# A convolution and expert kernel on one core: scatters, first step and small operations placed otherwise

## The chip, the core and the metric

One core of a Trainium2 chip runs the whole kernel. A core has five engines, each with an instruction list of its own that it takes in order: TensorE (PE: matmuls, and PEld: the loads of their weights), VectorE (DVE), ScalarE (ACT), GpSimd (POOL) and SyncE (SP), which here issues loads and stores. [...] The metric is the time of the kernel in device microseconds (us), as the median of several executions.

## The reference

The input `x` (8 × 3584 × 192) is weighted over the last seven rows, with softmax weights for each of eight groups of 24 columns. Each of the 28672 rows of the result goes through the one of eight experts that has the largest gate product.

```python
def _attn_ref(x, weight_gen) -> np.ndarray:
    w = weight_gen - np.max(weight_gen, axis=-1, keepdims=True)
    w = np.exp(w)
    w = w / (np.sum(w, axis=-1, keepdims=True) + 1e-09)
    ...
    out = np.einsum('bshk,bskhg->bshg', w, x_unf)

def _moe_ref(x, w_gate, w1, w2) -> np.ndarray:
    logits = x @ w_gate
    expert_idx = np.argmax(logits, axis=1)
    ...
    for e in range(E):
        mask = expert_idx == e
        xe = x[mask]
        h = np.maximum(xe @ w1[e], 0.0)
        ye = h @ w2[e]
        out[mask] = gate_w[mask, None] * ye
```

## The kernel before

The kernel has two halves that run side by side. The **producing half** takes the rows in 16 chunks of 14 rows per partition (1792 rows). For each chunk VectorE makes the softmax weights (`soft_a`: maximum and difference, L324 and L326; ScalarE's exponential, L328; `soft_b`: sums, reciprocal and product, L361 to L370) and the convolution (13 pairs of halves, L387 and L392). The rows are then written as a high and a low part: ScalarE the high (`tops`, L401), VectorE the low (`halves`, L414). TensorE transposes them (`turn`, L428, 42 transposes; ScalarE copies them to `xt`, L429) and multiplies them by the gate (`products`, L437, 42 small matmuls). VectorE finds the expert of each row (`route1`, L451 to L464) and the number of rows for each expert of each partition, `cnt`; TensorE adds these up (`counts`, L479 and L480, with ScalarE's exponential of the gate values, `lg`, L478), and VectorE makes the position of each row in the experts' lists (`route2`, L503 to L519; `ge` is the sum of the exponentials and becomes the gate factor) and the tables of blocks (L542 and on). POOL then scatters the 14 rows of each partition to those positions in the memory `scr` (L491).

The **consuming half** takes blocks of 256 or 128 rows of one expert out of `scr`. SP loads the expert's weights `wa` (L622, L623) and `wb` (L654), the block's rows transposed, `xb` (L631), and their numbers, `mt` (L639). A block has four or two **steps**: TensorE makes 10 matmuls of the first product (L675 to L679), ScalarE `hh` from it (relu, L682), and the rest `hl` is made by VectorE (L692) or by TensorE and ScalarE (L689, L690). The second product (L709) follows some steps later, then ScalarE's `y` (L717) and POOL's scatter to the output (L718).

Ahead of both lies the preparation of the weights (to about 125 us): `gram` and `scales` find a scale for each expert, `high`, `split` and `low_sum` write the weights in two parts, and SP stores them to `wsa` and `wsb` (L288, L292, L296), from where the blocks load them. `first_rows` issues `xb` and `mt` of the very first block, `first_weights` its `wa`.

A planner that is written out by hand sets the order of the instructions: `produce` walks through slots `o` of each chunk `c` and adds the time `t` of VectorE's work; `consume` adds a step whenever its own time is due. `state["pe"]` is the time that the producing half takes on TensorE, which pushes the next step back. Tables such as `EARLY` and `THIRD` say in which slot each part comes. While the slots of chunk `c` run, the routing of chunk `c` − 1 is done; chunk numbers in this text count from 0. `PACED` is the first chunk whose scatters are tied to the steps: each such scatter waits for the `hh` of one step.

Of the kernel before, what the change touches and what calls it, by code (L numbers as in the profile page):

```python
# [19 lines left out]
E, F = 8, 1024  # L20
# [14 lines left out]
OPS = 2 * K - 1  # L35
WW = 7 * F + 2
WA, WB2 = 4160, 3136
PACED = 14
ZERO = dict(tops=0, halves=2, turn=3, per=1, products=8, route1=10, counts=12, route2=13, soft_a=11, soft_b=7, size=10)
FIRST = dict(tops=-1, halves=-1, turn=-1, per=6, products=-1, route1=2, counts=2, route2=3, soft_a=6, soft_b=10, size=8)  # L40
EARLY = dict(tops=-1, halves=1, turn=2, per=2, products=4, route1=6, counts=8, route2=9, soft_a=7, soft_b=10, size=11)
THIRD = dict(tops=-1, halves=0, turn=0, per=3, products=2, route1=3, counts=4, route2=5, soft_a=8, soft_b=10, size=11)
SECOND = dict(tops=-1, halves=-1, turn=-1, per=6, products=-1, route1=-1, counts=-1, route2=0, soft_a=6, soft_b=10, size=8)
END = 2.1
LONE = {1: 6, 2: 2}
WB = 4
SB = 5
# [33 lines left out]
def conv_moe_kernel(ctx: ExitStack, tc: tile.TileContext, x, wgen, wg_in, w1, w2, out):  # L81
# [151 lines left out]
    def prep_units():  # L233

        sqs = {}

        def gram(e):
            po = ps2.tile([P, 512], F32, name="po")
            for k in range(2):
                hi = ptiles[e][:, k, :].bitcast(BF16).rearrange("p (f z) -> p f z", z=2)[:, :, 1]  # L240
                for q in range(NW // P):
                    m = hi[:, q * P:q * P + P]
                    PE.matmul(po[:, k * P:k * P + P], lhsT=m, rhs=m, start=k == 0 and q == 0, stop=k == 1 and q == NW // P - 1)
            sqs[e] = po

        def norms(e):
            sq = small.tile([P, 2], F32, name="wsq", bufs=3)
            for k in range(2):
                gj = small.tile([P, P], F16, name="gj")
                A.activation(out=gj, in_=sqs[e][:, k * P:k * P + P], func=AF.Relu, scale=2.0 ** (-2 * (LW1, LW2)[k]), accum_out=sq[:, k:k + 1])  # L250
            PE.matmul(sqs[e][:, 256:258], lhsT=onef, rhs=sq, start=True, stop=True)

        def scales(e):
            with tc.high_priority(offset=PRIO3):
                scale_of(sqs.pop(e)[:, 256:258], ws[:, 2 * e:2 * e + 2], wi[:, 2 * e:2 * e + 2], V, WTOP)

        wts, stored = {}, {}

        def high(e, k):
            t = ptiles[e]  # L260
            sc = ws[:, 2 * e + k:2 * e + k + 1]
            si = small.tile([P, P], F32, name="si", bufs=3)
            A.activation(out=si, in_=idf, func=AF.Copy, scale=sc)
            wt = stg[0].tile([P, 2 * NW + 2], F16, name="wt", bufs=SB)
            A.activation(out=wt[:, 0:NW], in_=t[:, k, :], func=AF.Copy, scale=sc)
            if k:
                A.activation(out=wt.bitcast(F32)[:, NW:NW + 1], in_=wi[:, 2 * e:2 * e + 1], func=AF.Copy, scale=wi[:, 2 * e + 1:2 * e + 2])
            wts[e, k] = wt, si

        def low(e, k):  # L270
            t = ptiles[e]
            wt, si = wts.pop((e, k))
            for q in range(3):
                p1 = ps1.tile([P, 512], F32, name="p1")
                PE.matmul(p1, lhsT=si, rhs=t[:, k, q * 512:q * 512 + 512], start=True, stop=False)  # L275
                PE.matmul(p1, lhsT=negi, rhs=wt[:, q * 512:q * 512 + 512], start=False, stop=True)
                A.activation(out=wt[:, NW + q * 512:NW + q * 512 + 512], in_=p1, func=AF.Copy)
            stored[e, k] = wt

        def low_sum(e, k):  # L280
            wt, _ = wts.pop((e, k))
            V.scalar_tensor_tensor(out=wt[:, NW:2 * NW], in0=ptiles[e][:, k, :], scalar=ws[:, 2 * e + k:2 * e + k + 1], in1=wt[:, 0:NW], op0=ALU.mult, op1=ALU.subtract)
            stored[e, k] = wt

        def store(e, k, l):
            wt = stored.pop((e, k)) if l else wts[e, k][0]
            if k:
                SP.dma_start(out=wsb[e, :, l * NW:(NW, 2 * NW + 2)[l]], in_=wt[:, l * NW:2 * NW + 2 if l else NW])  # L288
                if l and e + WB < E:
                    prep_load(e + WB)  # L290
                return
            SP.dma_start(out=wsa[e, :, (1, 3)[l] * F:(2, 4)[l] * F], in_=wt[:, l * NW:l * NW + F])  # L292
            for y in range(2 - l):
                for z in range(2):
                    o = (2, 0)[l] * F + 512 * z
                    SP.dma_start(out=wsa[e, 64 * y:64 * y + 64, o:o + 512], in_=wt[64 * z:64 * z + 64, l * NW + F:(l + 1) * NW])  # L296

        units, last = [(TW0, 0, gram, 0), (0, 1.1, norms, 0), (0, 0.0, scales, 0), (0, 1.9, high, 0, 0), (0, 0, store, 0, 0, 0), (TW0 + TWE, 0, gram, 1)], None
        for e in range(E):
            if e:  # L300
                units += [(0, 1.9, high, e, 0), (0, 0, store, e, 0, 0)]
            if last:
                units += [(0, 2.0, low, *last), (0, 0, store, *last, 1)]
            if e + 1 < E:
                units.append((0, 1.1, norms, e + 1))
            units += [(0, 2.1, high, e, 1), (0, 0, store, e, 1, 0), (0, 2.0, low, e, 0), (0, 0, store, e, 0, 1)]
            if e + 2 < E:
                units.append((TW0 + (e + 2) * TWE, 0, gram, e + 2))
            if e + 1 < E:
                units.append((0, 0.0, scales, e + 1))  # L310
            last = (e, 1)
        units[-1:-1] = [(0, 0, first_rows)]
        units += [(0, 0.0, low_sum, *last), (0, 0, store, *last, 1), (0, 0, first_weights)]
        for t, cost, f, *args in units:
            yield t, cost, f.__name__
            f(*args)
            if f is norms or f is scales:
                state["norm"] = f is norms


    def soft_a(c):
        wgt, n = tin[c]["wgt"], WID[c] * H
        mx = small.tile([P, T * H], F32, name="mx")[:, 0:n]
        V.tensor_reduce(out=mx, in_=wgt, axis=AX.X, op=ALU.max)  # L324
        yield 1.0
        V.tensor_tensor(out=wgt, in0=wgt, in1=mx.unsqueeze(2).to_broadcast([P, n, K]), op=ALU.subtract)  # L326
        with tc.high_priority(offset=PRIO2):
            A.activation(out=wgt, in_=wgt, func=AF.Exp)  # L328
        yield 1.0

    def size_a(c):
        xin = tin[c]["xin"]
# [110 lines left out]
    def route1(s):  # L443
# [14 lines left out]
        with tc.high_priority(offset=PRIO2):  # L458
# [5 lines left out]
            V.tensor_tensor_scan(out=inc.rearrange("p e t -> p (e t)"), data0=scm[n].rearrange("p e t -> p (e t)"),  # L464
                                 data1=oh.rearrange("p e t -> p (e t)"), initial=0.0, op0=ALU.mult, op1=ALU.add)
            cnt = small.tile([P, E], F16, name="cnt")
            if s < 2:
                V.tensor_copy(out=cnt, in_=inc[:, :, n - 1])
            else:
                A.activation(out=cnt, in_=inc[:, :, n - 1], func=AF.Copy)  # L470
# [26 lines left out]
    def route2(s):  # L497
# [3 lines left out]
        with tc.high_priority(offset=PRIO2):  # L501
            ge = small.tile([P, n], F32, name="ge")
            V.tensor_reduce(out=ge, in_=lg, axis=AX.X, op=ALU.add)  # L503
            if s < 2:
                V.tensor_scalar(out=ge, in0=ge, scalar1=1e-9, scalar2=d["sx"][:, 1:2], op0=ALU.add, op1=ALU.mult)
            else:
                A.activation(out=ge, in_=ge, func=AF.Copy, bias=1e-9)
                A.activation(out=ge, in_=ge, func=AF.Copy, scale=d["sx"][:, 1:2])
# [258 lines left out]
    def produce():  # L767
# [19 lines left out]

        for _ in soft_a(0):
            pass
        for e in range(WB):  # L790
            prep_load(e)
        load_chunk(1)
# [4 lines left out]
        for c in range(nchunk + 1):  # L797
# [4 lines left out]
            for o in range(-1, OPS + 1 + LONE.get(c, 0) // 2):  # L802
# [15 lines left out]
                if c == 2 and o == -1:  # L818
                    ta = prepare(1e9, ta)
                    state["begin"] = t + TLOAD  # L820
                    for d in soft_a(c):
                        t += d
                    ta += 0.9
                if c == 1 and o == -1:
                    for d in soft_b(c):
# [9 lines left out]
                    turn_ = turn(c - 1)  # L835
                for _ in range(at_o["per"]):
                    if turn_ and next(turn_, 0):
                        state["pe"] += 0.9
                        ta += 1.1
                if o == at_o["products"] and c:  # L840
                    products_ = products(c - 1)
                for _ in range(1 if at_o in (EARLY, THIRD) else 2):
                    if products_ and (r := next(products_, 0)):
                        state["pe"] += r
                if o == 4 and c == 0:
                    prep_gate()
                if o == 11 and c == 0:
# [11 lines left out]
                if c + 1 < nchunk and c != 1:  # L859
                    if o == at_o["soft_a"]:  # L860
                        ta += 1
                        for d in soft_a(c + 1):
                            t += d
                            yield t
                    if o == at_o["soft_b"] and c:
                        soft_ = soft_b(c + 1)
                    while soft_ and (d := next(soft_, None)) is not None:
# [7 lines left out]
                        yield t  # L875
                if o == at_o["counts"] and c:
                    counts(c - 1)
                if o == at_o["route2"] and c == 1:
                    ta = scaled(t, ta)
                if o == at_o["route2"] and c:  # L880
# [12 lines left out]
    def consume():  # L893
# [14 lines left out]
        for n, (s, i, b, bs) in enumerate(todo):  # L908
# [12 lines left out]
            for k in range(blk.steps):  # L921
                with tc.high_priority(offset=PRIO):
                    step(blk, k)
                if clears:
                    clear()
                for _ in range(2 if paced and paced[0][0] < nchunk - 1 else len(paced[:1])):
                    z, col, pos = paced.pop(0)
                    info = mybir.DependencyInfo(mybir.DependencyClass.Sync, mybir.DependencyReason.DATA)
                    tc.add_manual_dep(scatter(z, col, pos), blk.relu.name, info, reason="one per step")
# [78 lines left out]
```

## Time and profile before

| | us |
|---|---|
| median of 3 executions | 1214.31 |
| lowest and highest | 1212.57, 1219.76 |
| profiled execution, its time | 1218.53 |
| profiled execution, its span | 1216.8 |

| engine | busy us in the span | share |
|---|---|---|
| TensorE, matmuls | 1131.4 | 93% |
| TensorE, weight loads | 1016.4 | 84% |
| VectorE | 1048.1 | 86% |
| ScalarE | 696.6 | 57% |
| GpSimd | 776.5 | 64% |

The span goes from the first to the last instruction; the time has 1.7 us more around it. Weight loads and matmuls of TensorE overlap. [...] The busy shares are averages over stages: preparation up to about 125 us, both halves together up to about 1000 us, and then the remaining blocks alone.

### The profile page before, as it was taken

The page shows a single profiled execution, that of the slowest core. Times are in us where ns is not written, and L with a number is a line of the kernel's source. Part 1 is how long each engine was busy: PE and PEld are TensorE (multiplying, and loading weights), DVE is VectorE, ACT ScalarE, POOL GpSimd, SP SyncE. Part 2 cuts the span into 40 slices and gives each one's busy share as a digit, 9 for nine tenths or more (in the row PEclk, how much of TensorE's full clock was granted, in tenths as well). Part 3 has the DMA queues.
Part 4 walks back from the last instruction along what each step waited for, and adds up shares of the span by engine and source line. Part 5 has one row for each costly group of instructions (what it writes and reads, how often), then busy time and mean ns, then how long its engine had stood idle before and what let it go on. Part 6 is the DMA issues. An engine that isn't in the chain of part 4 may idle for free.

```text
span 1216.8 us, 31890 instructions
## 1 busy us (share of the span) xinstructions
PE 1131.4 (93%) x12127; PEld 1016.4 (84%) x12127; DVE 1048.1 (86%) x1408; ACT 696.6 (57%) x1394; POOL 776.5 (64%) x587
## 2 busy tenths in 40 slices
PE   4777888889999999999999999999999999999997
PEld 2343777778888888989989999999999999899997
DVE  7999899998999999999999999999999995333332
ACT  3877557667686776755546364554636445343342
POOL 1434572757587878886868788787878885522222
PEclk9889799999999999999999999999999999999999
DMA  9986999899998999999999999999999998999994
GB/s 299 302 266 226 293 313 325 238 325 250 252 290 230 268 278 242 294 268 267 298 273 305 252 311 273 274 289 279 304 262 269 241 291 249 292 289 263 252 241 160
DMA packets 214064, 331.43 MB, mean 272 GB/s; under 512 B 138382, under 2 KB 157951, under 8 KB 211856
## 3 DMA queue, kind: packets, MB, share of 16 engines
q1 hardware_dynamic: 191056, 282.70, 84.7%
q0 software_dynamic: 21696, 44.99, 13.0%
q8 instruction: 97, 1.59, 0.6%
q10 hardware_dynamic: 1152, 1.64, 0.4%
q14 instruction: 63, 0.52, 0.2%
HBM read 246.39 MB, written 60.83 MB: 252 GB/s over the span
## 4 chain that ended last, share of the span: by engine, by line
DVE 43%; PE 32%; DMA 9%; issue 8%; ACT 5%; SPq 1%; POOL 1%; POOLq 0%; ACTq 0%; DVEq 0%
PE po L709 13%; DVE tmp L387 12%; DVE acc L392 12%; DVE hl L692 7%; PE p L675 3%; PE p L679 3%; PE p L677 3%; PE p L678 3%; PE p L676 3%; PE p L275 3%; DVE acc L387 2%; DVE rows L414 2%; DMA wa<-wsa 2%; DMA out_dram<-y,mt 2%; DMA xb<-scr 1%
## 5 line engine op out<-in xcount | busy, mean ns | idle before, releaser
L718 POOL DMA_INDIRECT out_dram<-y,mt x228 | 343.6, 1507 | 218.9 <-ACT y L717 147.2
L491 POOL DMA_INDIRECT scr<-rows,pos x224 | 338.2, 1510 | 145.9 <-issue 55.5
L682 ACT ACTIVATE hh<-p 128x512 f16<-128x512 f32 x456 | 270.8, 599 | 261.3 <-PE p L679 243.8
L709 PE MATMUL po<-wb,hh 128*128 128x192 f16 x3648 | 361.4, 247 | 6.1 <-ACT hh L682 5.6
L692 DVE SCALAR_TENSOR_TENSOR hl<-p,hh 128x512 f16<-128x512 f32 x322 | 215.1, 677 | 122.7 <-ACT hh L682 122.6
L709 PEld LDWEIGHTS <-hh 128*128 128x128 f16 x3648 | 308.5, 98 | 12.1 <-ACT hh L682 9.4
L387 DVE TENSOR_TENSOR tmp<-xin,wgt 128x1344 f32<-128x1344 f32 x192 | 292.2, 1546 | 1.2
L392 DVE TENSOR_TENSOR acc<-acc,tmp 128x1344 f32<-128x1344 f32 x192 | 292.4, 1544 | 0.4
L675 PE MATMUL p<-xb,wa 128*128 128x256 f16 (+1 forms) x960 | 257.9, 269 | 11.1 <-DMA xb<-scr 4.9
L677 PE MATMUL p<-xb,wa 128*128 128x256 f16 (+1 forms) x960 | 258.0, 269 | 0.0
L678 PE MATMUL p<-xb,wa 128*128 128x256 f16 (+1 forms) x960 | 258.0, 269 | 0.0
L676 PE MATMUL p<-xb,wa 128*128 128x256 f16 (+1 forms) x960 | 257.9, 269 | 0.0
L679 PE MATMUL p<-xb,wa 128*128 128x256 f16 (+1 forms) x960 | 257.9, 269 | 0.0
L709 PE MATMUL po<-wb,hl 128*128 128x192 f16 x1824 | 226.2, 247 | 14.7 <-ACT hl L690 14.7
L709 PEld LDWEIGHTS <-hl 128*128 128x128 f16 x1824 | 161.1, 98 | 26.3 <-ACT hl L690 18.6
L676 PEld LDWEIGHTS <-wa 128*128 128x128 f16 x960 | 94.4, 98 | 22.9 <-issue 5.7
L675 PEld LDWEIGHTS <-wa 128*128 128x128 f16 x960 | 94.4, 98 | 13.6 <-issue 6.1
L679 PEld LDWEIGHTS <-wa 128*128 128x128 f16 x960 | 94.5, 98 | 10.3
L677 PEld LDWEIGHTS <-wa 128*128 128x128 f16 x960 | 94.4, 98 | 10.3
L678 PEld LDWEIGHTS <-wa 128*128 128x128 f16 x960 | 94.4, 98 | 10.3
L690 ACT ACTIVATE hl<-p 128x512 f16<-128x512 f32 x134 | 80.5, 601 | 38.2 <-PE p L689 37.7
L429 ACT ACTIVATE xt<-p 128x1024 f16<-128x1024 f16 x96 | 83.0, 934 | 7.9 <-PE p L428 7.0
(145 smaller groups left out, 1082.5 us busy)
## 6 DMA issues: line engine op xcount, KB each, us to landing
wb<-wsb SPq DMA_DIRECT2D x120, 768.5 KB
wa<-wsa SPq DMA_DIRECT2D x120, 768.0 KB
xin<-in_x_dram SPq DMA_DIRECT2D x15, 1344.0 KB
wa<-wsa SPq DMA_DIRECT2D x120, 128.0 KB
wgt<-in_weight_gen_dram SPq DMA_DIRECT2D x16, 392.0 KB
wa<-in_moe_w_dram SPq DMA_DIRECT2D x8, 768.0 KB
wa<-in_moe_w_dram SPq DMA_DIRECT2D x8, 512.0 KB
wsa<-wt SPq DMA_DIRECT2D x16, 256.0 KB
```

What stands on the lines that cost most here:

```text
L387: V.tensor_tensor(out=t[:, a:b, :].rearrange("p t (h g) -> p (t h) g", g=G), in0=xv, in1=wv, op=ALU.mult)
L392: V.tensor_tensor(out=acc[:, a:b, :], in0=acc[:, a:b, :], in1=t[:, a:b, :], op=ALU.add)
L491: i = raw(GP.indirect_dma_start(scri, bass.IndirectOffsetOnAxis(ap=pos[:, t:t + 1], axis=0), rows_t[s % 3].bitcast(I32)[:, t, 0:RW // 2], ...
L675: PE.matmul(o, lhsT=wt[:, F + fs:F + fs + P], rhs=xv[:, 0, :], start=i == 0, stop=False)
L676: PE.matmul(o, lhsT=wt[:, F + fs:F + fs + P], rhs=xv[:, 1, :], start=False, stop=False)
L677: PE.matmul(o, lhsT=wt[:, 3 * F + fs:3 * F + fs + P], rhs=xv[:, 0, :], start=False, stop=False)
L678: PE.matmul(o, lhsT=wt[:, 2 * F + fs:2 * F + fs + P], rhs=xv[:, 2, :], start=False, stop=False)
L679: PE.matmul(o, lhsT=wt[:, fs:fs + P], rhs=xv[:, 2, :], start=False, stop=i == self.each - 1)
L682: self.relu = raw(A.activation(out=hh, in_=p1, func=AF.Relu, scale=1.0 - 2.0 ** -11 if self.via[k] else 1.0))
L692: V.scalar_tensor_tensor(out=hl, in0=p1, scalar=0.0, in1=hh, op0=ALU.max, op1=ALU.subtract)
L709: PE.matmul(o, lhsT=h[:, js], rhs=w2, start=(f == 0 and j % 2 == 0 and not part and w == 0), stop=part == 1 and f == NF - 1 and (j % 2 == ...
L718: i = raw(GP.indirect_dma_start(out, bass.IndirectOffsetOnAxis(ap=self.mt[:, j, 1:2], axis=0), y, None, bounds_check=N - 1, oob_is_err=False))
```

## The change

Line numbers after the change are 1 to 13 higher (L437 is L442, L675 is L680, L491 is L496). The change has five parts:

1. `PACED` goes from 14 to 9, and each step takes one scatter (before, two a step for chunk 14 and one for chunk 15; chunks 9 to 13 had their 14 scatters in a row).
2. The copy to `cnt` and the factor on `ge` are VectorE's up to chunk 5; before, up to chunk 1.
3. ScalarE's exponential of the softmax is taken out of `soft_a` and issued one slot later, for the slots of chunk 2 two slots later (`soft_e`).
4. `first_rows` is issued ahead of the stores of the last expert's second group, and no longer at the end of them.
5. In the slots of chunk 2 the transposes and products of chunk 1 cost TensorE nothing in the plan, the counts cost 7.0, and a `yield` behind the transposes lets a step be issued there.

```diff
-PACED = 14
+PACED = 9
+GATE = 7.0
@@ prepare
         for e in range(E):
+            if e == E - 1:
+                units.append((0, 0, first_rows))
             if e:
                 units += [(0, 1.9, high, e, 0), (0, 0, store, e, 0, 0)]
...
-        units[-1:-1] = [(0, 0, first_rows)]
@@ soft_a
         V.tensor_tensor(out=wgt, in0=wgt, in1=mx.unsqueeze(2).to_broadcast([P, n, K]), op=ALU.subtract)
+        yield 1.0
+
+    def soft_e(c):
+        wgt = tin[c]["wgt"]
         with tc.high_priority(offset=PRIO2):
             A.activation(out=wgt, in_=wgt, func=AF.Exp)
-        yield 1.0
@@ route1
-            if s < 2:
+            if s < 6:
                 V.tensor_copy(out=cnt, in_=inc[:, :, n - 1])
@@ route2
-            if s < 2:
+            if s < 6:
                 V.tensor_scalar(out=ge, in0=ge, scalar1=1e-9, scalar2=d["sx"][:, 1:2], op0=ALU.add, op1=ALU.mult)
@@ produce
                     for d in soft_a(c):
                         t += d
+                    soft_e(c)
...
                     if turn_ and next(turn_, 0):
-                        state["pe"] += 0.9
+                        state["pe"] += 0.9 if c != 2 else 0.0
                         ta += 1.1
+                if c == 2 and o == -1:
+                    yield t
...
                     if products_ and (r := next(products_, 0)):
-                        state["pe"] += r
+                        state["pe"] += r if c != 2 else 0.0
...
+                    if o == at_o["soft_a"] + (2 if c == 2 else 1):
+                        soft_e(c + 1)
...
                     counts(c - 1)
+                    if c == 2:
+                        state["pe"] += GATE
@@ consume
-                for _ in range(2 if paced and paced[0][0] < nchunk - 1 else len(paced[:1])):
+                for _ in paced[:1]:
                     z, col, pos = paced.pop(0)
```

What this does to the order of the instructions, at three places. On TensorE, around the very first step of the first block; before, `p_1336` is the result of that step, `rows_141` are the rows of chunk 1, and `wg` is the gate:

```order
L428 MATMUL p_1280<-idh,rows_141 128x128
L437 LDWEIGHTS xt
L437 MATMUL route<-wg_149,xt 128x16
...
L437 MATMUL route<-wg_150,xt 128x16
L675 LDWEIGHTS wa_143
L675 MATMUL p_1336<-xb_145,wa_143 128x256
...
L479 LDWEIGHTS tri
L479 MATMUL route<-cnt,tri 128x8
```

And after, where the first step's result is `p_1285` and the second's `p_1407`:

```order
L433 MATMUL p_1280<-idh,rows_141 128x128
L680 LDWEIGHTS wa_143
L680 MATMUL p_1285<-xb_145,wa_143 128x256
...
L442 LDWEIGHTS xt
L442 MATMUL route<-wg_149,xt 128x16
...
L442 MATMUL route<-wg_150,xt 128x16
L680 LDWEIGHTS wa_143
L680 MATMUL p_1407<-xb_145,wa_143 128x256
...
L484 MATMUL route<-cnt,tri 128x8
```

One step (10 matmuls) has moved from behind the 42 products of chunk 1 to ahead of them, and a second step now stands between the products and the counts.

On ScalarE at the same place, before (the `hh` of `p_1336` is the first step's):

```order
L429 ACTIVATE xt<-p_1280 128x256
L449 ACTIVATE fac<-sx,wi 128x1
L682 ACTIVATE hh<-p_1336 128x512
L478 ACTIVATE lg<-lg,fac 128x112
L682 ACTIVATE hh<-p_1480 128x512
```

And after:

```order
L434 ACTIVATE xt<-p_1280 128x256
L687 ACTIVATE hh<-p_1285 128x512
L454 ACTIVATE fac<-sx,wi 128x1
L687 ACTIVATE hh<-p_1407 128x512
L483 ACTIVATE lg<-lg,fac 128x112
L687 ACTIVATE hh<-p_1449 128x512
```

The exponential `lg` of chunk 1 has moved behind the `hh` of the second step.

On SP at the end of the preparation, before (a TENSOR_LOAD reads a table into a register, for the address of the rows):

```order
L292 DMA wsa<-wt 128x1024
L296 DMA wsa<-wt 64x512 x4
L288 DMA wsb<-wt 128x1538
L288 DMA wsb<-wt 128x1536
L616 TENSOR_LOAD tb3False
...
L631 DMA_TRANSPOSE xb_145<-scr 128x3x256
...
L639 DMA mt_146<-scr 128x2x2
L292 DMA wsa<-wt 128x1024
L296 DMA wsa<-wt 64x512 x2
L288 DMA wsb<-wt 128x1538
...
L622 DMA wa_143<-wsa 128x3072
```

And after:

```order
L621 TENSOR_LOAD tb3False
...
L636 DMA_TRANSPOSE xb_145<-scr 128x3x256
...
L644 DMA mt_146<-scr 128x2x2
L293 DMA wsa<-wt 128x1024
L297 DMA wsa<-wt 64x512 x4
L289 DMA wsb<-wt 128x1538
L289 DMA wsb<-wt 128x1536
L293 DMA wsa<-wt 128x1024
L297 DMA wsa<-wt 64x512 x2
L289 DMA wsb<-wt 128x1538
...
L627 DMA wa_143<-wsa 128x3072
```

Seven stores have moved from ahead of the first `xb` and `mt` to behind them; `wa` follows the last store in both.

## Rows read from the trace of the kernel before

**Rows 1.** table by stretches: busy PE, PEld, DVE, ACT, POOL; clock; DMA

```profile
600.00:750.00 150.00, 147.97 (x1665) 139.34 (x1662) 148.31 (x195) 77.39 (x160) 119.54 (x75) 1.00 1.04 278
998.00:1217.00 219.00, 209.46 (x2320) 198.18 (x2317) 81.65 (x162) 87.20 (x191) 74.37 (x75) 0.99 0.93 251
```

**Rows 2.** waits of VectorE, 100 to 998 us: total, times, longest

```profile
DVE rows L516 <- ACT ge L508: 2.4, 1, 2.4
```

**Rows 3.** waits of TensorE, 100 to 300 us

```profile
PE po L709 <- ACT hl L690: 10.8, 7, 3.2
...
PE p L675 <- DMA xb<-scr: 3.6, 3, 2.2
```

**Rows 4.** ScalarE's timeline: start, duration, what [idle before, releaser]

```profile
222.31 0.86 ACT L328 ACTIVATE wgt<-wgt 128x784 f32<-128x784 f32 x1 [4.44 <-DVE wgt L326]
...
978.12 0.21 ACT L507 ACTIVATE ge<-ge 128x14 f32<-128x14 f32 x1 [6.35 <-DVE ge L503]
```

**Rows 5.** VectorE's timeline at three places

```profile
228.07 0.96 DVE L361 TENSOR_REDUCE sm<-wgt 128x112 f32<-128x784 f32 x1
...
584.42 2.07 DVE L414 SCALAR_TENSOR_TENSOR rows<-acc,sx,rows 128x1792 f16<-128x1792 f32 x1
...
655.57 2.07 DVE L414 SCALAR_TENSOR_TENSOR rows<-acc,sx,rows 128x1792 f16<-128x1792 f32 x1
```

**Rows 6.** TensorE's timeline behind the ge of chunk 14

```profile
979.30 0.82 PE L709 MATMUL po<-wb,hh 128*128 128x192 f16 x8
```

**Rows 7.** waits of TensorE, 998 us to the end

```profile
PE p L675 <- DMA xb<-scr: 1.3, 1, 1.3
```

**Rows 8.** TensorE's timeline around the first step

```profile
126.89 1.05 PE L437 MATMUL route<-wg,xt 128*128 128x16 f16 x32
128.19 0.50 PE L437 MATMUL route<-wg,xt 128*128 128x16 f16 x10 [0.25 <-ACT xt L429]
130.83 0.39 PE L675 MATMUL p<-xb,wa 128*128 128x256 f16 x1 [2.14 <-DMA wa<-wsa]
...
132.94 0.21 PE L479 MATMUL route<-cnt,tri 128*128 128x8 f16 x1
...
136.08 0.27 PE L675 MATMUL p<-xb,wa 128*128 128x256 f16 x1
```

**Rows 9.** VectorE's timeline around the first step

```profile
128.73 0.39 DVE L451 TENSOR_REDUCE lg<-route 128x112 f32<-128x224 f32 x1 [0.76 <-PE route L437]
...
131.19 0.17 DVE L468 CAST cnt<-inc 128x8 f16<-128x8 f32 x1
131.27 1.55 DVE L387 TENSOR_TENSOR acc<-xin,wgt 128x1344 f32<-128x1344 f32 x1
134.13 0.27 DVE L503 TENSOR_REDUCE ge<-lg 128x14 f32<-128x112 f32 x1 [1.32 <-ACT lg L478]
134.44 0.23 DVE L505 TENSOR_SCALAR ge<-ge,sx 128x14 f32<-128x14 f32 x1
```

**Rows 10.** table by stretches, columns as in rows 1, around the first step

```profile
124.00:135.00 11.00, 8.61 (x92) 7.24 (x93) 8.51 (x18) 5.43 (x9) 2.31 (x4) 0.50 1.01 290
```

**Rows 11.** timeline of TensorE (PE matmul, PEld weight load) near 72 us

```profile
72.77 0.17 PE L479 MATMUL route<-cnt,tri 128*128 128x8 f16 x1 [3.26 <-DVE cnt L468]
...
72.78 0.10 PEld L480 LDWEIGHTS <-ones 128*128 128x128 f16 x1 [3.33 <-issue]
```

**Rows 12.** SP's timeline of DMA issues ahead of the first wa

```profile
111.32 1.11 SPq L296 DMA_DIRECT2D wsa<-wt  x2
113.07 0.34 SPq L292 DMA_DIRECT2D wsa<-wt  x1
...
124.87 0.35 SPq L622 DMA_DIRECT2D wa<-wsa  x1
```

**Rows 13.** POOL's timeline, row scatters of chunk 12, first and last of fourteen

```profile
839.86 0.96 POOL L491 DMA_INDIRECT scr<-rows,pos  x1 [3.04 <-DVE pos L519]
...
863.99 1.76 POOL L491 DMA_INDIRECT scr<-rows,pos  x1 [0.30 <-issue]
```

More of the change, by code (lines that the diff above doesn't have):

```diff
@@ L789, in produce @@
             pass
+        soft_e(0)
         for e in range(WB):
```

## Prediction

> **What bounds the kernel now.** I read the table by stretches first, then who waits on each engine, then the timeline of the few places that the change touches. In the middle of the kernel two engines are near their limit: VectorE is busy for 148.31 of 150 us and TensorE for 147.97; from 998 us VectorE falls to 81.65 of 219 us while TensorE stays at 209.46 [rows 1]. Who waits says which of the two leads before 998 us. VectorE waits for almost nothing between 100 and 998 us: its largest wait is one of 2.4 us for ScalarE [rows 2]. TensorE waits for others: 10.8 us between 100 and 300 us on `hl` of ScalarE, up to 3.2 us at a time [rows 3], and ScalarE stood there behind an exponential that waited for VectorE, 4.44 us at one place [rows 4]. Later one chunk takes 71.15 us from one low part of the rows to the next (L414 at 584.42 and 655.57) [rows 5], of which TensorE, with its 2.03 idle us in 150 [rows 1], loses one. So VectorE's one in-order list sets the time up to 998 us, TensorE is nearly as full, and what is won on TensorE before 300 us meets a VectorE that comes no sooner. The last tie between the two that I find is ScalarE's `ge` of chunk 14 (L507), which waited 6.35 us for VectorE up to 978.12, with ScalarE's list behind it [rows 4]; TensorE went on at 979.30 without a stop [rows 6]. From there it waits once, 1.3 us for an `xb` [rows 7].
>
> The working rule: a delay of VectorE's list before 978 us passes to the end, less what TensorE has in hand at 978 us; a gain of TensorE alone does not.
>
> **The first step ahead of the products (extra yield, costs of the planner).** Before, the 42 products on `xt` ran from 126.89 to 128.69, and only then came the first step (10 matmuls, L675 to L679), which waited 2.14 us for `wa` and ran from 130.83 to the counts at 132.94 [rows 8]. Now the step stands ahead of the products. TensorE then stands still from the end of the transposes, about 126.9, until `wa` lands, and the products, for which VectorE waits (L451 began at 128.73, 0.04 us after their end [rows 9]), stand behind it. [...] From L451 to the end of L387 VectorE has 4.09 us of work (128.73 to 131.27, and 1.55); before, it then waited 1.32 us for `lg` of ScalarE, up to 134.13 [rows 9]. [...] **VectorE is then +3.6 us late (2.0 to 3.8).**
>
> [...]
>
> **First block's rows sooner (SP).** Two register reads, `xb` and `mt` now stand ahead of the last expert's second group of stores, with `wa` behind all of them as before. The only idle time that they can fill is ahead of the store at 113.07, 0.64 us after the one before it (111.32 and 1.11); then SP is busy up to the last store, and `wa` was issued at 124.87 [rows 12]. The same instructions in another order end 0.6 us sooner (0 to 0.9). `xb` itself gains nothing by landing earlier, since `wa` ends last. The 0.6 us are in the term above.
>
> **Counts and factors on VectorE up to chunk 5.** Four CAST and four TENSOR_SCALAR more on VectorE, 0.17 and 0.23 us by their rows; the instruction behind the CAST began 0.08 us after its start [rows 9]. With 0.04 us of issue on top as the other end: 4 × (0.08 to 0.21) + 4 × (0.11 to 0.27) = 0.8 to 1.9 us; I take 1.4, nearer to the rows' own durations. Nothing hides it, as VectorE has no gaps. In return `ge` no longer goes by way of ScalarE, where it cost VectorE its largest wait, 2.4 us ahead of L516 [rows 2]: that goes whole, the value being VectorE's own. **Net −1.0 us.** ScalarE loses twelve instructions and its waits ahead of them, which helps TensorE, but by the rule is not kept.
>
> **Exponentials one or two slots later.** On ScalarE one to three `hh` more stand ahead of each exponential, so most of TensorE's 10.8 us on `hl` [rows 3] should go. VectorE must still get its exponential in time. The closest place is the one at 222.31, ended at 223.17, whose sums VectorE reads at 228.07: 4.9 us [rows 4, 5]. Two steps more ahead of it are about 4.2 us (two times 2.11), and ScalarE had waited 4.44 us there anyhow [rows 4], in which they fit. Cost nothing; if that cover were gone, VectorE would lose up to 2 us once. TensorE's early gain, up to 14 us with the 3.6 us on `xb` [rows 3], turns into waits for VectorE within a chunk or two.
>
> **Pacing of the row scatters, chunks 9 to 15.** Fourteen scatters in a row took POOL from 839.86 to 865.75, 25.9 us [rows 13]; one per step of 2.1 us they take 29 us, and output scatters pass between them. The scale chain of the next chunk (L190 to L193), in the same queue, now stands behind the twelfth scatter, before behind the fourteenth and six output scatters, so at about the same time. Who could wait is the load of `xb`. The last chunk, paced one per step in the kernel before too, had one such wait, 1.3 us [rows 7]; so +1.3 is one end. The other: TensorE was idle for 2.03 of 150 us [rows 1], some 6 us over chunks 9 to 15, and bursts may have caused a quarter of that. I take 0 (−1.5 to +1.3). [...]
>
> **The sum.** VectorE's list at chunk 14: +3.6 + 1.4 − 2.4 = +2.6 us (2.0 + 0.8 − 2.4 = +0.4 to 3.8 + 1.9 − 2.4 = +3.3). The order leaves as many `hh` ahead of `ge` of chunk 14 as before, so TensorE has in hand there what it had: more than nothing, as it did not stop, and at most the 1.2 us from 978.12 to 979.30 [rows 4, 6]; I take 0.6. **+2.0 us (−0.8 to +3.3).** The profiled execution lasted 1218.53 us, so 1220.5 by it; that execution is 4.22 us above the median of 1214.31, so **1216.3** against the median.
>
> **Rivals.**
> (A) VectorE is not held, because `wa` lands during the transposes or the products get past. For it: the stores on SP are moved. Against it: `wa` was issued last on SP and still is. Then −1.0 − 0.6 at most: 1212.7 to 1214.3.
> (B) Slower. The step ahead of the products makes VectorE wait for `wa` itself, one for one, and the stores that were put behind `xb` now run just ahead of that load. Each us that `wa` lands after 130 us adds one. Waits for a load of up to 2.2 us were seen (`xb` [rows 3]); twice that on top gives +2.0 + 2.2 to 4.4, so 1218.5 to 1221. It decides from 1 us on, and is a measurable loss only from about 10 us on, which nothing shows.
> (C) TensorE keeps what it wins before 300 us. That needs a VectorE with time in hand, against which its 148.31 of 150 us speak [rows 1]; for it, that the planner orders later chunks anew. The waits on `hl` and `xb`, 10.8 + 3.6 [rows 3], would give 14.4: 1199.9, and half of it 1207.
> (D) It does nothing, since VectorE's delay is taken up by what TensorE has in hand: 1214.3.
>
> **How the numbers follow.** Chances: the forecast (1213.5 to 1217.6) 0.52, A and D together 0.25, B 0.13, C 0.10. The range goes from 1208, just short of C's half, to 1221, the end of B. About 1% (12 us) is what a measurement of this kernel tells from no change: its three runs lie 0.6% apart. Faster by more: most of C, 0.08. Slower by more: B far beyond its bounds, 0.05. Within it: 0.87.
>
> **What would show it.** L451 of chunk 1 begins about 133.6 in place of 128.73, and its wait for TensorE grows from 0.76 to some 5.6 us; VectorE's wait for `lg` and its 2.4 us wait are gone; TensorE's waits on `hl` fall by most of 10.8 us and come back as waits between 200 and 500 us; L414 comes 2 to 3 us later in the middle of the kernel, with the same period. The forecast is wrong if L451 begins before 131 (then A), if `wa` lands after 133 (then B), or if TensorE is idle for 8 us less over the whole span (then C).

## The result and the profile after

The changed kernel takes 1228.92 us (median of four executions, 1223.43 to 1233.09) against 1214.65 us before (now four executions as well): 1.0106 times as long, with a 95% interval of 1.0063 to 1.015. That is 14.3 us slower, where I had forecast 2 us, and outside my range. The profiled execution took 1233.09 us, the longest of the four, with a span of 1231.4 us. Its preparation ended some 4 us later than that of e1 below, which has the same order up to there: the first `wa` was issued at 129.00 us, in e1 at 124.79. Its single times are read with that in mind. Where executions spread widely, from e9 on, the ratios leave out those more than 1.5% above the fastest of their kernel.

VectorE's waits after (line, releaser, total us, times, longest), 100 to 998 us. The wait of [rows 2] is gone, and another has come:

```profile
DVE lg L456 <- PE route L442: 7.7, 2, 6.5
DVE hl L697 <- ACT hh L687: 1.7, 1, 1.7
```

The same on TensorE, 100 to 300 us, which answers to [rows 3]. The waits on `hl` have become fewer and longer, and in sum stay as they were:

```profile
PE po L714 <- ACT hl L695: 10.5, 3, 6.0
...
PE p L680 <- DMA wa<-wsa: 4.4, 1, 4.4
PE p L680 <- DMA xb<-scr: 3.5, 3, 2.2
```

The first step on TensorE's timeline after, which answers to [rows 8]. The step now waits for `wa` first, and the products of chunk 1 come behind it, at 137.01:

```profile
134.90 0.39 PE L680 MATMUL p<-xb,wa 128*128 128x256 f16 x1 [4.41 <-DMA wa<-wsa]
...
137.01 1.31 PE L442 MATMUL route<-wg,xt 128*128 128x16 f16 x42
...
141.04 0.17 PE L484 MATMUL route<-cnt,tri 128*128 128x8 f16 x1 [0.68 <-DVE cnt L473]
```

VectorE's timeline at that place, which answers to [rows 9]: it waits 6.55 us where it had waited 0.76, and no longer waits for `lg` ahead of `ge`.

```profile
138.36 0.39 DVE L456 TENSOR_REDUCE lg<-route 128x112 f32<-128x224 f32 x1 [6.55 <-PE route L442]
...
140.82 0.17 DVE L473 CAST cnt<-inc 128x8 f16<-128x8 f32 x1
140.90 1.55 DVE L392 TENSOR_TENSOR acc<-xin,wgt 128x1344 f32<-128x1344 f32 x1
142.37 0.26 DVE L508 TENSOR_REDUCE ge<-lg 128x14 f32<-128x112 f32 x1
142.66 0.23 DVE L510 TENSOR_SCALAR ge<-ge,sx 128x14 f32<-128x14 f32 x1
```

The largest change stands elsewhere. SP's waits after, 600 to 1000 us: the load of `xb` (L636) waited 18.7 us at one place for row scatters.

```profile
SPq L636 <- DMA scr<-rows,pos: 30.3, 4, 18.7
```

SP's timeline at that place, the end of the 18.7 us. The `wa` of the block was issued at 951.35 and 951.89, its `xb` at 971.53 only:

```profile
951.89 0.52 SPq L628 DMA_DIRECT2D wa<-wsa  x1
971.53 1.25 SPq L636 DMA_TRANSPOSE xb<-scr  x1
```

TensorE's longest wait, 600 to 1000 us, is the one for this `xb`:

```profile
PE p L680 <- DMA xb<-scr: 5.6, 1, 5.6
```

The table by stretches there (busy us of PE, PEld, DVE, ACT and POOL, granted clock of TensorE as a share of its full speed, share of the DMA engines, GB/s). TensorE is dry from 970 to 975 us, and then has five us at a granted clock of 0.52:

```profile
965.00:970.00 5.00, 4.54 (x62) 4.06 (x60) 4.97 (x5) 1.56 (x4) 4.31 (x3) 1.00 0.14 50
970.00:975.00 5.00, 0.00 (x0) 0.00 (x0) 4.83 (x11) 0.07 (x1) 3.86 (x4) 0.80 0.49 111
975.00:980.00 5.00, 4.91 (x29) 4.20 (x30) 5.00 (x6) 1.85 (x5) 3.81 (x3) 0.52 0.93 303
980.00:985.00 5.00, 5.00 (x57) 4.71 (x55) 3.33 (x4) 1.40 (x4) 0.00 (x0) 1.00 1.16 235
```

And POOL's timeline, where the scatters of that chunk, 13, stand; it answers to [rows 13]. The first of the fourteen is at 920.99, the twelfth ends at 955.05, then come the four instructions of the next chunk's scale chain, a scatter of 5.08 us, two output scatters and, at 968.18, the fourteenth. From the first to the end of the last 48.9 us go by, in place of 25.9 (chunk 13 of the kernel before, 911.00 to 936.89, took as long as chunk 12 in [rows 13]):

```profile
920.99 0.97 POOL L496 DMA_INDIRECT scr<-rows,pos  x1 [9.73 <-ACT y L722]
922.26 0.99 POOL L723 DMA_INDIRECT out_dram<-y,mt  x1 [0.30 <-issue]
923.55 0.98 POOL L723 DMA_INDIRECT out_dram<-y,mt  x1 [0.30 <-ACT hh L687]
...
953.77 1.28 POOL L496 DMA_INDIRECT scr<-rows,pos  x1 [0.31 <-issue]
955.12 1.26 POOL L191 TENSOR_SCALAR eb<-sx 128x1 f32<-128x1 int32 x1
956.46 0.22 POOL L192 TENSOR_SCALAR ei<-eb 128x1 int32<-128x1 f32 x1
956.77 1.66 POOL L193 TENSOR_SCALAR sx<-ei 128x1 int32<-128x1 int32 x1
958.51 0.19 POOL L194 TENSOR_SCALAR sx<-sx 128x1 int32<-128x1 int32 x1
959.22 5.08 POOL L496 DMA_INDIRECT scr<-rows,pos  x1 [0.52 <-ACT xt L434]
964.61 1.69 POOL L723 DMA_INDIRECT out_dram<-y,mt  x1 [0.30 <-ACT xt L434]
966.60 1.28 POOL L723 DMA_INDIRECT out_dram<-y,mt  x1 [0.30 <-issue]
968.18 1.74 POOL L496 DMA_INDIRECT scr<-rows,pos  x1 [0.30 <-issue]
```

What counts here is in the brackets: behind the first scatter, POOL never stood idle for more than 0.5 us between two entries, and mostly for 0.3. The names behind the arrow are those of whatever signalled last. POOL had no gap to wait in; it was full.

The chain that ended last, 900 to 1000 us, by line, goes through that queue; in the kernel before it has lines of TensorE there for the most part:

```profile
by line: PE po L714 33.1%; DMA scr<-rows,pos 9.7%; PE p L680 7.3%; PE p L681 7.1%; PE p L682 7.1%; PE p L684 7.0%; PE p L683 7.0%; POOL scr L496 6.0%; DMA xb<-scr 3.2%; issue 2.8%; POOL out_dram L723 1.7%; POOL sx L193 1.7%; DVE acc L397 1.
```

### The profile page after: what moved, and what is told of

It is laid out like the page before. It is cut to its first block, busy times and chain, and to the rows that moved or that the text cites. A ratio compares the mean times of both kernels' runs of the same rounds, so it can differ in the third digit from the quotient of the medians.

```text
span 1231.4 us, 31979 instructions
## 1 busy us (share of the span) xinstructions
PE 1132.3 (92%) x12127; PEld 1017.3 (83%) x12127; DVE 1051.4 (85%) x1416; ACT 699.0 (57%) x1382; POOL 739.1 (60%) x587
## 4 chain that ended last, share of the span: by engine, by line
DVE 57%; PE 28%; DMA 6%; issue 4%; ACT 3%; POOL 1%; SPq 1%; DVEq 0%; POOLq 0%; ACTq 0%
DVE tmp L392 17%; DVE acc L397 16%; PE po L714 12%; DVE hl L697 8%; DVE acc L392 3%; DVE rows L419 3%; PE p L680 3%; PE p L684 3%; PE p L683 3%; PE p L681 3%; PE p L682 3%; PE p L276 2%; DMA wa<-in_moe_w_dram 1%; DMA wa<-wsa 1%; DVE mx L326 1%
## 5 line engine op out<-in xcount | busy, mean ns | idle before, releaser
L496 POOL DMA_INDIRECT scr<-rows,pos x224 | 354.1, 1581 | 179.1 <-issue 46.6
L723 POOL DMA_INDIRECT out_dram<-y,mt x228 | 303.0, 1329 | 232.9 <-ACT y L722 171.3
L680 PE MATMUL p<-xb,wa 128*128 128x256 f16 (+1 forms) x960 | 258.2, 269 | 18.0 <-DMA xb<-scr 9.5
L680 PEld LDWEIGHTS <-wa 128*128 128x128 f16 x960 | 94.5, 98 | 20.6 <-issue 9.6
```

Of the source, the lines that this page charges most:

```text
L496: i = raw(GP.indirect_dma_start(scri, bass.IndirectOffsetOnAxis(ap=pos[:, t:t + 1], axis=0), rows_t[s % 3].bitcast(I32)[:, t, 0:RW // 2], ...
L680: PE.matmul(o, lhsT=wt[:, F + fs:F + fs + P], rhs=xv[:, 0, :], start=i == 0, stop=False)
L723: i = raw(GP.indirect_dma_start(out, bass.IndirectOffsetOnAxis(ap=self.mt[:, j, 1:2], axis=0), y, None, bounds_check=N - 1, oob_is_err=False))
```

## The experiments

Two theories stood against each other after the result. P: pacing fills POOL's queue, the load of chunk 13's rows waits, and TensorE runs dry. V: only VectorE's list is late, by the wait at the first step, and the stop at 975 us takes up time that TensorE would have waited for VectorE anyway.

**e1: the changed kernel without pacing.**

```diff
-PACED = 9
+PACED = 14
...
-                for _ in paced[:1]:
+                for _ in range(2 if paced and paced[0][0] < nchunk - 1 else len(paced[:1])):
```

> The changed kernel with the row scatters as before (chunks 9 to 13 in bursts, 14 two a step). Theory P (pacing fills POOL's queue, the load of chunk 13's first rows waits 18.7 us, and TensorE runs dry at 975 us): no such wait, TensorE has no stop of over 2 us between 600 and 1000 us, and 5 to 8 us come back against the changed kernel, to about 1222. Theory V (VectorE's list is what is late, the stop at 975 us only takes up what TensorE would have waited for anyway): within 2 us of the changed kernel, about 1228.

1221.6 us, 1.0048 times the kernel before (1.0034 to 1.0061), so 7 us came back. In its trace TensorE's waits from 600 to 1000 us, the two kinds below, hold no wait for a load:

```profile
PE po L714 <- ACT hh L687: 3.1, 3, 1.2
PE po L714 <- DVE hl L697: 2.1, 3, 0.7
```

**e2: the kernel before with pacing alone** (the two edits of e1 the other way).

> The kernel before with the paced scatters of chunks 9 to 15 alone. Theory P: SP waits over 10 us for row scatters ahead of one first load, TensorE stops for some us, and the time is 4 to 8 us above the kernel before, about 1220. Theory V: within 2 us of the kernel before.

1223.38 us against 1215.3, 1.0064 (1.005 to 1.0077): 8.1 us slower by this part alone. SP's longest wait for row scatters and TensorE's longest, 600 to 1000 us, are the same two:

```profile
SPq L632 <- DMA scr<-rows,pos: 27.4, 3, 18.7
```

```profile
PE p L676 <- DMA xb<-scr: 5.0, 1, 5.0
```

Theory P holds for this part, and V falls for it.

**e3: the changed kernel with the products ahead of the first step again.**

```diff
-                        state["pe"] += 0.9 if c != 2 else 0.0
+                        state["pe"] += 0.9
...
-                if c == 2 and o == -1:
-                    yield t
...
-                        state["pe"] += r if c != 2 else 0.0
+                        state["pe"] += r
...
-                    if c == 2:
-                        state["pe"] += GATE
```

> The changed kernel with the planner's costs and the yield of chunk 2 as before, so that the products of chunk 1 stand ahead of the first step again. Both theories: VectorE's wait of 6.55 us for the products falls below 1.5 us, and its list is 4 to 5 us sooner from 140 us on. Theory V: all of it comes back, about 1224.5. Theory P: the stop at 975 us stays, since it hangs on POOL and not on VectorE; 2 to 5 us come back, 1224 to 1227.

1222.48 us, 1.0057 (1.0043 to 1.007). 6.4 us came back, with the stop of TensorE still there (5.3 us). So the two losses add up: the stop at 975 us does not swallow VectorE's delay. The chain from VectorE's positions over POOL and SP to TensorE starts that much later: the `xb` of that place was issued at 961.68 here and at 971.53 in the changed kernel, and only some 4 us of this difference are the later preparation.

**e4: the changed kernel with the exponential of chunk 1 at once.**

```diff
-                    if o == at_o["soft_a"] + (2 if c == 2 else 1):
+                    if o == at_o["soft_a"] + (2 if c == 2 else 1 if c else 0):
```

> The changed kernel with the exponential of chunk 1 alone issued at once, as before. Both theories: VectorE's wait of 1.44 us for it near 62 us goes, low part of chunk 0 about 1.8 us sooner; time 1.5 to 2 us below the changed kernel, about 1227.

1227.52 us (1222.12 to 1231.78), 1.0094 (1.0068 to 1.0121). VectorE's wait of 1.44 us at 62 us was gone in its trace; the 1.4 us in the medians are within the intervals, so the size stays unproven. The wait is not there in every execution either: with the same exponential it was 0.45 us in e6, 0.67 in e7 and none in e1.

**e5: the kernel before with the step's part alone** (the edits of e3 the other way).

> The kernel before with the planner's costs and the yield of chunk 2 alone, so that the first step stands ahead of chunk 1's products. Theory S (the products' wait for the first wa is the price): VectorE's wait for the products about 6 us in place of 0.8, its list 4 to 5 us late from 140 us on, time 5 to 6 us above the kernel before, about 1220.5. Theory N (this is small, the 6.3 us that the changed kernel without pacing still loses come from the other three parts): within 2 us of the kernel before.

1221.75 us, 1.0053 (1.0039 to 1.0066): 6 us by this part alone. The time is that of theory S. The executions lie between 1216.61 and 1225.54, and the profiled one is the shortest of the six, 0.7 us above the kernel before. Its wait was smaller than expected:

```profile
DVE lg L452 <- PE route L438: 4.5, 2, 3.8
```

VectorE also did not wait for `ge` ahead of L517 (L516 before), where it had waited 2.4 us in [rows 2]. Its last low part of chunk 14 began at 943.32 us, as in the trace of the kernel before (943.31). So this trace fits its own short time, but a wait that goes with the 6 us of the median was not seen in e5. It was seen in e1, which has the same step and took 6.3 us more than the kernel before:

```profile
DVE lg L456 <- PE route L442: 7.6, 2, 6.5
```

**e6: without pacing (as e1) and without the extra yield, the plan's costs kept.**

```diff
-                if c == 2 and o == -1:
-                    yield t
```

> The changed kernel without pacing (1221.6) and without the extra yield, the planner's other costs kept: the products of chunk 1 come first, then two steps, then the counts. Theory S: the wait for the products is below 1.5 us; VectorE may wait 1 to 2 us for the counts or lg behind the second step; time 1215 to 1217.5. Theory G (the costs of the plan, which move steps and counts all along, are the price): no more than 1.5 us come back, 1220 to 1222.

1220.56 us, 1.0034 (1.0021 to 1.0047). That is within G's range, and 3 us above S's. VectorE's waits, 100 to 998 us, tell why:

```profile
DVE ge L508 <- ACT lg L483: 3.4, 1, 3.4
DVE lg L456 <- PE route L442: 3.0, 2, 2.3
```

The wait has mostly moved: with two steps between the products and the counts, `lg` stands behind the second `hh`. The two sums, 6.4 us here and 7.6 in e1, differ by 1.2 us; the times differ by 1.0, and by 1.7 if each is taken against the kernel before on its own chip. So most of the price stays without the yield. The two traces fit the reading that every step costs that stands ahead of something VectorE waits for; no run has the yield without the plan's costs.

**e7: two scatters a step.**

```diff
-                for _ in paced[:1]:
+                for _ in paced[:2]:
```

> The changed kernel (1228.9) with two scatters a step from chunk 9 on. Theory T (each scatter waits for its step, and with the output scatters in between POOL needs over 45 us for the fourteen): the fourteen are done in some 30 us, SP's longest wait for row scatters falls from 18.7 to under 8 us, TensorE does not stop for xb, time 1221 to 1224. Theory O (output scatters among the row scatters are the cause, tied or not): SP still waits over 12 us and the time stays over 1226.

1222.66 us, 1.0052 (1.0039 to 1.0065 of before), the same as e1 without any pacing. The fourteen scatters of chunk 13 took 31.2 us, and TensorE did not wait for `xb`. SP's longest wait between 600 and 1000 us:

```profile
SPq L636 <- DMA scr<-rows,pos: 4.9, 1, 4.9
```

Tying the scatters to steps costs nothing that shows; one a step is what costs.

**e8: counts and factors, and the exponentials from chunk 2 on, alone** (the kernel before with `s < 6` and `soft_e`, chunk 1 as before).

> The kernel before with two parts alone: counts and factors on VectorE up to chunk 5, and the exponentials one or two slots later from chunk 2 on. By the prediction's terms VectorE gains 2.4 us at its wait near 277 us and pays 1.4 us: 1213.5 to 1214.5, which is 1 us below the kernel before. Rival: the later exponentials leave TensorE's early gain in part, 1209 to 1212.

1216.47 us against 1215.9, 1.0003 (0.9992 to 1.0015). My two small terms of this pair, −1.0 us and 0, lie within that, and so does no effect at all.

**e9, e13, e17 and e18: which place in POOL's queue costs.** The kernel before with pacing, but three scatters in the first step of a chunk:

```diff
-                for _ in paced[:1]:
+                for _ in paced[:3 if len(paced) == T else 1]:
```

> The kernel before with pacing alone (1223.4), except that the first step of a paced chunk takes three scatters, so that all fourteen come within twelve steps and stand ahead of the next chunk's scale chain on POOL; the output scatters stay among them. Theory C (the last two scatters behind the scale chain are what the load of chunk 13's rows waits for): SP's longest wait falls from 18.7 to under 8 us, no stop of TensorE for xb, time 1215 to 1218. Theory O (the output scatters among them are enough): SP waits 10 us or more, time over 1220.

> The kernel before with pacing alone (1223.4), except that the first step of a paced chunk takes three scatters, so that all fourteen come within twelve steps and stand ahead of the next chunk's scale chain on POOL; the output scatters stay among them. In the run of this kernel on the slow chip SP's longest wait was 3.9 us. Theory C (the last two scatters behind the scale chain are what the load of chunk 13's rows waits for): no stop of TensorE for xb, time 1215 to 1218, level with the kernel before. Theory O (the output scatters among them are enough): over 1220.

> The kernel before with pacing alone, but three scatters in the first step of a paced chunk, so that the fourteen stand ahead of the next scale chain on POOL; the output scatters stay among them. Beside e18 on the same chip. Theory C (the last two scatters behind the scale chain are the price): level with the kernel before, within 2 us. Theory O (the output scatters among them are enough): 5 us or more above, as e18.

> The kernel before with pacing alone, the control for e17 on the same chip: 6 to 10 us above the kernel before under both theories, SP's longest wait for row scatters about 18 us if the chip is one on which the kernel before takes 1215 us; less of both if it is a slower one, since the blocks then come later.

From e9 on the runs fell on chips on which all kernels, that of before too, took 35 to 65 us longer and spread more, so only ratios on one chip are read. Three scatters in the first step: 0.9966 (0.9887 to 1.0046), 0.9997 (0.9936 to 1.0057) and 1.0013 (0.9971 to 1.0055), three times level with the kernel before. Pacing alone beside the last of them: 1.0061 (1.0027 to 1.0094), as in e2. SP's longest wait for row scatters was 8.9 us in e17, and among TensorE's waits from 600 to 1000 us there was none for `xb`; in e18 it was 17.6 us, with a stop of TensorE (first line e17, the others e18):

```profile
SPq L632 <- DMA scr<-rows,pos: 8.9, 1, 8.9
...
SPq L632 <- DMA scr<-rows,pos: 18.4, 2, 17.6
...
PE p L676 <- DMA xb<-scr: 3.8, 1, 3.8
```

The output scatters are among the row scatters in both. That speaks for theory C, the last two scatters behind the scale chain; the intervals of e17 and e18 overlap, so by the times it is likely rather than settled. The traces say more. In the four traces with such a stop, it was 13 to 14 us shorter than SP's wait: 5.6 of 18.7 us in the changed kernel, 5.0 of 18.7 in e2, 5.3 of 18.9 in e3, 3.8 of 17.6 in e18. A wait of 8.9 us (e17) or 4.9 us (e7) is below that, and there was no stop.

**e10 and e15: the first block's rows sooner, alone.**

```diff
+            if e == E - 1:
+                units.append((0, 0, first_rows))
...
-        units[-1:-1] = [(0, 0, first_rows)]
```

> The kernel before with the first block's rows issued sooner alone. By the prediction wa lands 0.6 us sooner and nothing else moves: 0 to 0.6 us below the kernel before. Rival (the stores behind it come late and hold wa): up to 2 us above.

> The kernel before with the first block's rows issued sooner alone: 0 to 0.6 us below the kernel before by the prediction. Rival (the stores behind it come late and hold wa): up to 2 us above.

1.0013 (0.9945 to 1.0081) and 0.9996 (0.995 to 1.0043): nothing that shows, either way; an effect of 0.6 us could not show in these intervals.

**e11 and e14: the first step behind the counts.**

```diff
-AV, TLOAD, SLOW = 4.0, 12.0, 0.5
+AV, TLOAD, SLOW = 4.0, 15.0, 0.5
```

> The kernel before with the begin of the first block 3 us later in the plan, so that the first step stands behind the counts of chunk 1, and lg of chunk 1 ahead of the first hh: the opposite of the changed kernel. Theory S: VectorE waits neither for wa nor for lg there; its waits of 0.8 and 1.3 us shrink to about 1 us in all, its list is 1 to 1.5 us sooner, time 1213.5 to 1215.5. Rival (TensorE's early work is what counts, and it loses a step's time): 1 to 3 us above the kernel before.

> The kernel before with the begin of the first block 3 us later in the plan: first step behind the counts of chunk 1, lg ahead of the first hh, the opposite of the changed kernel. Theory S: VectorE waits there for about 1 us in all in place of 2.1, and the time is 1 to 1.5 us below the kernel before. Rival (TensorE's early work is what counts): 1 to 3 us above.

1.0157 (1.001 to 1.0305) and 1.0022 (0.9968 to 1.0076): the first interval lies above one, the second, with more executions, does not; inconclusive. VectorE's waits for the products and `lg` there were 1.3 us in all, as expected, but no gain in time follows from these runs.

**e12 and e16: the same, with the parts of e8.**

> The same, with counts and factors on VectorE up to chunk 5 and the exponentials later from chunk 2 on. Theory S: 1 us below the one before it, 1212.5 to 1215. Rival: as the kernel before, 1215 to 1217.

> The kernel with the step behind the counts, with counts and factors on VectorE up to chunk 5 and the exponentials later from chunk 2 on. Theory S: 1 to 2.5 us below the kernel before. Rival: as the kernel before.

0.9948 (0.9863 to 1.0033) and 0.9984 (0.9933 to 1.0034): not faster by anything that these runs can tell. None of these kernels was shown to be faster than the kernel before.

## Why the prediction was wrong

**Pacing, the step that failed.** I took 0 (−1.5 to +1.3); it costs 8.1 us (e2). The sentence that failed is that the scale chain "now stands behind the twelfth scatter [...] so at about the same time". The chain did come at about the same time (953.04 before, 955.12 after). But I asked only when it comes, and not what stands behind it: the last two of the fourteen scatters, for which the next load of rows waits. It also took 29 us from the steps' pace for the fourteen, while POOL's own entries set the time: fourteen row scatters, the output scatters and the chain, with 0.3 to 0.5 us between two, took 48.9 us. The bound from the last chunk, 1.3 us, was no bound, since no scale chain follows there. No run shows the other end, −1.5 us, which was my estimate of what bursts cost TensorE: with two scatters a step the time is that of e1, which has the bursts (1222.66 and 1221.6 us). In the kernel before the burst took 25.9 us, and no load waited for it; I did not look up when the load that reads these rows can go, some 31 us after the first scatter (952.4, where SP's wait begins, less 920.99). The trace gives most of the price, as an estimate: in the changed kernel 5.6 us dry and 5 us at 0.52 of the clock, in which 2.4 us of work are lost, together 8.0 us; in e2 5.0 us dry and 5 us at 0.66, or 1.7 us, together 6.7 us against the 8.1 measured.

**The first step ahead of the products: right in kind, too small.** VectorE was to be 3.6 us late at `ge`. No run shows that term; the trace of the changed kernel shows this in its place: the wait for products and `lg` went from 0.76 and 1.32 us [rows 9] to 6.55 us at chunk 1, and at chunk 2 it waited 1.2 us more for the products (7.7 us in two): 5.7 us in place of 3.6. Of the difference, 0.9 us is the wait at chunk 1, which grew by 5.8 us where I had taken 4.9 (from 0.76 to 5.6), with a `wa` that did not land sooner against the transposes, and 1.2 us that the products of the next chunk are late as well, which I had not looked for. The step itself took the 2.11 us of [rows 8] again (134.90 to 137.01), at the granted clock of [rows 10], 0.50. In time the part costs 5.9 us alone (e5, by medians that spread over 9 us) and 6.4 us inside the change (e3). How long the wait is depends on the execution: 6.5 us in the changed kernel, e1 and e7, but 3.9 in e4 and 3.8 in e5.

**First block's rows sooner.** The 0.6 us did not come. The preparation itself was about 4 us later in this execution (first `xb` at 118.40 on SP, then stores up to 127.83, `wa` at 129.00), and `wa` was again on its way for 5 us after it had been issued. In the traces of e1 to e8 `wa` was issued at times between 122.4 and 127.2 us, and the two orders of the stores are mixed among them, so 0.6 us can't be told from them. Alone the part shows nothing (e15). In e1, with the same order as the changed kernel, the first step began at 130.71 us; so the start at 134.90, which by itself is the sign that I had set for B, is mostly the late preparation.

**Counts, factors, exponentials.** The wait of 2.4 us went whole, as predicted, and the sum of these parts is nought to within 2 us (e8). The 2.4 us were likely too much to put into the sum as a gain: I had read them off one execution, and at the same place, with `ge` still going by way of ScalarE, VectorE waited 1.2 us in e2 and not at all in e5. I had the exponential of chunk 1 at nothing and looked only at a later one (222.31 us); VectorE waited up to 1.44 us for it (e4).

**The rule about VectorE** held as far as traces and times can be compared: e3 against the changed kernel, and e6 against e1, follow VectorE's waits to within a us or so. In e5 it holds for the profiled execution alone, as said there. TensorE had no early gain to keep; its waits on `hl` did not even fall, where I had expected most of 10.8 us to go. But the rule was not the whole: a third resource, POOL's queue, had its own way to stop TensorE, over SP's load. Rival B named a late load as the mechanism, though the wrong one, and D, A (the products came behind the step, at 137.01) and C are out.

The sum by the runs: 8.1 (e2) + 5.9 (e5) + 0.6 (e8) = 14.6 us, against 14.3 measured. My terms were 0, +3.6 and −1.0, less 0.6 that TensorE had in hand. That the sum comes out to 0.3 us is luck: each of the three is known to 1.5 us or so only, they were taken on two chips, and the 14.3 us themselves lie between 8 and 18.

## What to carry to other kernels

When transfers are spread over a longer time, look up who reads what the last one writes, and add up every entry of the issuing queue up to that last one, also those of other work that the new order puts ahead of it; the pace of what triggers them is only the lower bound (29 us by the steps here, where 48.9 went by). A queue without gaps in its timeline is a resource of its own, however harmless its busy share (60 to 64% here). And here work that waited for a load (4.41 us for `wa`), put ahead of what a saturated engine was waiting for, held that engine up: VectorE waited 6.55 us where it had waited 0.76.

## What the runs showed of the hardware

In the trace of the changed kernel a scatter's time on POOL goes with what VectorE does meanwhile. All 67 scatters that began after 1020 us, when the convolution is over, took 1.0 us at most. Of the 180 between 560 and 990 us, 113 took over 1.2 us, and 83 of these ended 0.2 to 0.4 us after the end of an `hl` on VectorE; ahead of that `hl` stood one of VectorE's large operations, in 64 of them one of the convolution. By chance some 10% would end so near to an `hl`, as an estimate: 191 of them in these 430 us, with a window of 0.2 us behind each. The longest there is the one behind the scale chain, 5.08 us at 959.22 above; it ended at 964.30, and this `hl` at 963.95:

```profile
963.28 0.67 DVE L697 SCALAR_TENSOR_TENSOR hl<-p,hh 128x512 f16<-128x512 f32 x1
```

In e1 an output scatter at the same place took 4.97 us. So it looks as if POOL's scatters are held while VectorE runs these large operations, and POOL's queue is full because of it; no run tested this.

VectorE's period in the middle of the kernel was 71.2 us in e1, without pacing, and 71.5 in the changed kernel, without a wait. One of its instructions, an integer shift of eight numbers (L548), accounts for most of it: it took 0.41 us in place of 0.16 in all six places where a paced scatter had begun on POOL 0.5 us before it, as here:

```profile
778.56 0.41 DVE L548 TENSOR_SCALAR qi<-qi 1x8 int32<-1x8 int32 x1
```

In e1 no scatter ran beside that instruction in chunks 9 to 13, and it took 0.16.

After the stop of 5.6 us TensorE's granted clock was 0.52 of its full speed for the next 5 us; after the stop of 3.8 us in e18 it was 0.50 (990 to 995 us). In the changed kernel the matmuls of the step behind the stop took 0.42 us each and began 0.21 us apart (975.47 to 976.97); at a clock of 1.00, from 980.87 on, they took 0.27 us and began 0.11 us apart. So, as an estimate (0.48 of 5 us), the 5.6 us cost 2.4 us more, nearly half as much again.
